# A convolution's transform with 90 in place of 98 rows, positions loaded in two halves, four units moved into a gap

## Chip, cores, metric

One core of one Trainium2 chip. The metric is the device time of one execution in microseconds (us). The kernel before takes 2610.57 us (median of four runs, 2609.2 to 2613.86). Almost all executions of one kernel agree within 0.3%.

## The reference, cut

```python
# x, v: (4, 12544, 128); pos_emb: (12544, 64); tokens for the second block: 4 * 12544
h_mlp  = np.maximum(pos_emb @ w1, 0.0) @ w2
window = np.exp(-0.01 * np.arange(S))[:, None]          # float32
h_filt = h_mlp * window
u = x * v;  L = 2 * S
y = irfft(rfft(u, L) * rfft(h_filt, L), L)[:, :S]       # causal convolution, per channel
x2 = (x * y).reshape(B * S, D)
h = np.maximum(np.maximum(x2 @ m1, x2 @ m2), x2 @ m3)   # 128 -> 768
out = h @ m_out                                         # 768 -> 128
```

In float32 the window is exactly zero from s = 10398 on. The filter therefore lives in 82 of the 98 blocks of 128 positions (82 x 128 = 10496).

## The kernel before: the parts that matter here

Four stages follow one another on one core. **Start:** a small network of the positions makes the filter (`mlp_in`, `mlp_out`). **First transforms** (`first_halves`): of the filter (512 passes over `spec`), then of batch 0 (32 units). **Pair loop**: a second product, a multiplication in the frequency domain and a third product for each pair of rows, batch 0 and the filter together. **Tiles**: 128 tiles, 32 a batch, each a last transform (`yps`) and six blocks of the maxout part (`pa`, `pb`, `ops`); the convolution of the next batch runs in 192 numbered slots beside the tiles of this one (`conv_steps`). "Pass" below means one matmul of the trace with its weight load; a matmul of the program is recorded as two of them (a transpose as one).

```python
NA = 64
halves = ((0, NA), (NA, NB))              # NB = 98: 64 blocks of positions, then 34
hs = spec[0:NB]...                        # the filter's values land in rows 0..97 of spec
def mlp_in(i):                            # 16 calls
    for q in range(8):
        for hf, (lo_, hi_) in enumerate(halves):      # the halves alternate
            nc.tensor.matmul(ps[lo_:hi_, q*FO:(q+1)*FO],
                posv[64*hf:64*hf+64, P-1-8*i-q, 0:hi_-lo_],   # stationary: 64 rows x 64 or 34 columns
                w1_sb[64*hf:64*hf+64], start=(q == 0), stop=True, ...)
def first_halves(ps, lhs, dst, copy):
    ...                                   # lhs: 98 rows x 64 columns; f1: 98 rows x 98 columns a pass
def conv_steps(b, per_unit, per_pair, lag):
    for u in range(0, NU, 2): s = int(u * per_unit) + 6 ...    # [cut]
    for g in range(NK):                                        # 49 pairs
        s = s0 + int(g * per_pair)
        at(s + lag[4], g_third, b, g); at(s, g_second, g)
        at(s + lag[0], g_butterfly, g); at(s + lag[1], g_swap, g); ...
# called with per_unit 1.9, per_pair 2.3, lag (1, 2, 3, 4, 5)
```

One slot is one such block of `pa`, `pb` and `ops`.

## Time and profile before

| Stage (span of the profiled run) | from, us | to, us | length |
|---|---|---|---|
| until the filter transform starts | 0 | 53.19 | 53.2 |
| filter transform | 53.19 | 74.90 | 21.7 |
| batch 0's units | 74.90 | 143.62 | 68.7 |
| pair loop and gap, to the first `pa` | 143.62 | 363.86 | 220.2 |
| tiles with the convolutions beside them | 363.86 | 2605.8 | 2241.9 |

The boundaries are starts of instructions in TensorE's timeline. In a profile line `64*34 64x64` are the rows and columns of the stationary part, then those of the moving part and the output. The prediction below shows the lines that its reading rests on. Two timeline lines (start, length, engine, line, what, count):

```profile
36.03 1.98 PE L262 MATMUL ps<-w_sb,specH 64*64 64x64 f32 x32
...
53.19 21.88 PE L124 MATMUL ps<-f,spec 98*64 98x98 f32 x512 [0.58 <-issue]
```

A run of 32 products of the positions takes 1.92 us from its start to the next instruction's, 60 ns a pass; longer runs take 56. The filter transform takes 42.7 ns a pass. The trace's first record of the clock is a rise at about 29.0 us. Ahead of that record the profile shows full clock for want of anything else. That the clock was half until then can be seen from one pair of passes in between, the `pw` product at 23.97 us: it took 0.75 us, and 0.45 us in run onepos (below), whose clock had risen at 22.9 us. So the products up to 29.0 us ran at half clock, 56 ns a pass, and they kept that pace after the rise.

### The profile page before, as it was taken

Reading aid. Unit: us, or ns where it says so; the run is one execution under the profiler, and the core shown is the slowest. Engines: PE = TensorE matmul, PEld = TensorE weight load, DVE = VectorE, ACT = ScalarE, POOL = GpSimd, SP = SyncE. Lnnn points to the kernel's source line nnn. Section 1 sums busy time; section 2 is a strip of 40 time slices with the busy share of each in tenths; the row PEclk is TensorE's granted clock in tenths of the full one; section 3 lists DMA queues with packets and bytes.
Section 4 is the critical chain, followed back from the end, with each engine's and each line's share of the span. In section 5 each row is a group of like instructions: output and inputs, shape, how many; then the busy total and the mean of one; then the engine's idle time right before and its main releaser. Section 6 shows DMA issues by size and latency. Waiting matters only on the chain. (4 is left out here: it accounts for less than half of the span.)

```text
span 2605.8 us, 63932 instructions
## 1 busy us (share of the span) xinstructions
PE 2550.6 (98%) x26937; PEld 1559.7 (60%) x26937; DVE 1332.1 (51%) x2670; ACT 1084.9 (42%) x2064; POOL 61.4 (2%) x120
## 2 busy tenths in 40 slices
PE   6999989999999999999999999999999999999999
PEld 6877756666665656666656555666565554444444
DVE  5678843336666643335666653335666652222222
ACT  1478843334445433334444533334444442222222
POOL 1012200000000000000000000000000000000000
PEclk9999989999999999999999999999999999999999
DMA  6668864456888844456888754455887852222221
GB/s 158 151 191 258 257 165 105 104 143 182 233 223 227 237 122 103 103 137 178 225 224 227 224 141 109 104 133 159 235 225 220 227 165 60 54 63 60 55 61 35
DMA packets 441504, 409.19 MB, mean 157 GB/s; under 512 B 292314, under 2 KB 343168, under 8 KB 441088
## 3 DMA queue, kind: packets, MB, share of 16 engines
q1 hardware_dynamic: 313856, 311.26, 45.1%
q10 hardware_dynamic: 121920, 78.64, 10.5%
q0 software_dynamic: 5440, 15.21, 2.3%
q8 instruction: 211, 3.46, 0.6%
q14 instruction: 77, 0.63, 0.1%
HBM read 315.07 MB, written 89.92 MB: 155 GB/s over the span
## 5 line engine op out<-in xcount | busy, mean ns | idle before, releaser
L437 DVE TENSOR_TENSOR hid<-hid,pb 128x392 f32<-128x392 f32 x768 | 431.6, 562 | 700.1 <-PE pb L115 565.1
L434 ACT ACTIVATE hid<-pa 128x392 f32<-128x392 f32 x768 | 382.4, 498 | 708.0 <-PE pa L115 642.6
L115 PE MATMUL pa<-gt,w_sb 128*64 128x392 f32 x3072 | 641.1, 496 | 11.8 <-ACT hid L434 11.0
L115 PE MATMUL pb<-gt,w_sb 128*64 128x392 f32 x3072 | 636.8, 493 | 1.2 <-DVE hid L437 0.6
L115 PE MATMUL ops<-hid,wo_sb 128*64 128x392 f32 x3072 | 635.8, 492 | 0.1
L115 PEld LDWEIGHTS pb<-gt,w_sb 128*64 128x64 f32 x3072 | 218.2, 136 | 290.5 <-issue 203.4
L115 PEld LDWEIGHTS ops<-hid,wo_sb 128*64 128x64 f32 x3072 | 220.2, 137 | 285.7 <-issue 284.9
L115 PEld LDWEIGHTS pa<-gt,w_sb 128*64 128x64 f32 x3072 | 196.2, 137 | 161.0 <-issue 115.8
L345 DVE TENSOR_TENSOR xt<-xt,ht 128x512 f32<-128x512 f32 x196 | 135.5, 692 | 196.0 <-ACT xs L340 148.3
L115 PEld LDWEIGHTS yps<-f,zt 98*64 98x64 f32 x4096 | 189.8, 137 | 55.2 <-issue 46.1
L115 PEld LDWEIGHTS ps<-ab,wt 128*64 128x64 f32 x3136 | 178.8, 137 | 68.7 <-issue 36.4
L115 PE MATMUL ps<-ab,wt 128*64 128x128 f32 x3136 | 212.6, 276 | 3.2 <-DVE ab L356 3.2
L368 ACT COPY zs<-ps 128x512 f32<-128x512 f32 x196 | 115.3, 588 | 236.9 <-PE ps L115 225.8
L115 PE MATMUL ps<-spec,wt 128*64 128x128 f32 x3136 | 204.6, 273 | 0.0
L124 PEld LDWEIGHTS ps<-f,uT 98*64 98x64 f32 x4096 | 183.4, 137 | 35.2 <-issue 30.5
L115 PE MATMUL yps<-f,zt 98*64 98x98 f32 x4096 | 196.7, 248 | 7.6 <-DMA zt<-zd 7.6
L124 PE MATMUL ps<-f,uT 98*64 98x98 f32 x4096 | 192.1, 248 | 1.9 <-ACT uT L300 1.4
L115 PEld LDWEIGHTS ps<-spec,wt 128*64 128x64 f32 x3136 | 179.5, 137 | 18.9 <-issue 18.9
L425 DVE TENSOR_TENSOR gt<-yps,xT 128x392 f32<-128x392 f32 x128 | 72.5, 567 | 171.6 <-PE yps L115 169.0
L339 ACT ACTIVATE xs<-xt 64x512 f32<-64x512 f32 x196 | 123.2, 628 | 77.7 <-DVE xt L140 45.4
L356 DVE TENSOR_TENSOR ab<-xt 128x256 f32<-128x256 f32 x392 | 148.1, 419 | 1.7
L128 DVE COPY spec<-ps 128x392 f32<-128x392 f32 x128 | 71.3, 566 | 135.3 <-PE ps L124 135.3
(62 smaller groups left out, 1685.1 us busy)
## 6 DMA issues: line engine op xcount, KB each, us to landing
wt<-wt_const SPq DMA_DIRECT2D x147, 512.0 KB
ht<-hd SPq DMA_DIRECT2D x294, 256.0 KB
zd<-zs ACTq DMA_DIRECT2D x196, 256.0 KB
zt<-zd SPq DMA_DIRECT2D x128, 392.0 KB
ut<-in_xr_dram SPq DMA_DIRECT2D x128, 196.0 KB
ut<-in_vr_dram SPq DMA_DIRECT2D x128, 196.0 KB
wt<-wt_const SPq DMA_DIRECT2D x98, 256.0 KB
xT<-in_x_dram SPq DMA_DIRECT2D x512, 49.0 KB
```

The costliest lines, as they stand in the source:

```text
L115: nc.tensor.matmul(out[64 * h:64 * h + 64], lhsT[:, 64 * h:64 * h + 64], rhs, start=start, stop=stop, skip_group_check=True)
L124: nc.tensor.matmul(ps[64 * c:64 * c + 64, (2 * i + r) * NB:(2 * i + r + 1) * NB], lhs[i][:, 64 * r:64 * r + 64], f1[:, c * NB:(c + 1) * NB ...
L128: copy(dst, ps[:, 0:4 * NB].rearrange("p (s r k) -> p k r s", s=2, r=2))
L339: nc.scalar.mul(xs[0:64], xt[64:128], -1.0)
L345: nc.vector.tensor_tensor(out=xt[:], in0=xt[:], in1=hts[g][:, 0], op=ALU.mult)
L356: nc.vector.tensor_tensor(out=ab[:, :, q, :], in0=y[:, :, 0, :], in1=y[:, :, 1, :], op=op)
L368: nc.scalar.copy(zs[:].rearrange("p k f -> p (k f)"), ps[:])
L425: nc.vector.tensor_tensor(out=g[:], in0=ps[:, 0:N], in1=xTs.pop(i)[:].rearrange("d p n -> d (p n)"), op=ALU.mult)
L434: nc.scalar.activation(h[:], pa[:, 0:N], Relu)
L437: nc.vector.tensor_tensor(out=h[:], in0=h[:], in1=pb[:, 0:N], op=ALU.max)
```

## The change

Because the filter is short, a circular transform of 2 x 90 x 128 points is enough where 2 x 98 x 128 stood. So a batch has 45 pairs for 49, and a pass of the first transform 90 columns for 98. The filter network is made for 82 blocks only. The positions are loaded in two halves so that the first products can start early. The first four units of batch 1 are computed in the gap ahead of the first tile. The rest of the convolution steps are spread over the slots more widely. The copy of `G` is halved. The core of the diff:

```diff
+N1 = 90
+NH = 82
-    NK = NB // 2
+    NK = N1 // 2
-    halves = ((0, NA), (NA, NB))
+    halves = ((0, NA), (NA, NH))                      # second half: 34 -> 18 blocks
-    hs = spec[0:NB]...
+    hs = spec[0:NH]...                                # filter transform: 98 -> 82 rows
-                        ps[..., (2 * i + r) * NB:(2 * i + r + 1) * NB],
-                        lhs[i][:, 64 * r:64 * r + 64], f1[:, c * NB:(c + 1) * NB],
+                        ps[..., (2 * i + r) * N1:(2 * i + r + 1) * N1],
+                        lhs[i][:, 64 * r:64 * r + 64],
+                        f1[0:lhs[i].shape[0], c * N1:(c + 1) * N1],
-    for hf, (lo_, hi_) in enumerate(halves):
-        (...).dma_start(pos[64*hf:64*hf+64, 0:(hi_-lo_)*P], posT[:, lo_*P:hi_*P])
+    for a in (64, 0):
+        for hf, (lo_, hi_) in enumerate(halves):
+            (...).dma_start(pos... [:, 0:hi_-lo_, a:a+64], posT... [:, lo_:hi_, a:a+64])
-            beside = conv_steps(b + 1, 1.9, 2.3, (1, 2, 3, 4, 5)) if b + 1 < B else {}
+                done = 4 if b == 0 else 0
+                beside = conv_steps(b + 1, done, 2.0, (174 - 2.0 * (NU - done)) / NK,
+                                    (1, 2, 3, 4, 5))  # a pair every 2.62 or 2.44 slots
+            for u in range(4):                        # ahead of the first tile
+                u_first(u)
# cut: loads, multiplications and turns of these four units late in the pair loop;
#      buffers; the halved copy of G
```

## The prediction

> **What bounds the kernel now.** I read the page first, then the groups of TensorE instructions with shapes kept apart, then the stretches, then the timelines of three places. The page says that TensorE (PE) is busy nearly always, that the start is the exception, and that the granted clock dips only around one slice:
>
> ```profile
> PE 2550.6 (98%) x26937; PEld 1559.7 (60%) x26937; DVE 1332.1 (51%) x2670; ACT 1084.9 (42%) x2064; POOL 61.4 (2%) x120
> PE   6999989999999999999999999999999999999999
> PEclk9999989999999999999999999999999999999999
> ```
>
> Busy time alone proves little for pipelined matmuls, so I took start-to-start times. In the last quarter, where only the tiles of the maxout part run, a block of 4 passes of 392 columns starts every 0.66 us and a block of 32 passes of 98 columns takes 1.36 us:
>
> ```profile
> 2304.64 0.83 PE L115 MATMUL ops<-hid,wo_sb 128*64 128x392 f32 x4
> 2305.30 1.53 PE L115 MATMUL yps<-f,zt 98*64 98x98 f32 x32
> 2306.66 0.83 PE L115 MATMUL pa<-gt,w_sb 128*64 128x392 f32 x4
> ...
> ```
>
> So a pass costs 164.4 ns at 392 columns and 42.5 ns at 98. In the middle stage, 16 passes of 128 columns take 0.875 us (54.7 ns each; blocks at 897.61, 898.48, 899.36). Everything is columns times 1/2.4 ns plus 1 to 2 ns. From 380 us to the end the waits of PE add up to only 12.2 us, so there **columns removed from PE are time removed**. The stretches show where this is not so:
>
> ```profile
> 0.00:75.00 75.00, 54.85 (x1047) 52.90 (x1049) 42.98 (x114) 14.02 (x27) 9.37 (x21) 1.00 0.60 146
> 75.00:280.00 205.00, 197.83 (x2994) 162.73 (x2992) 151.52 (x320) 149.79 (x260) 33.89 (x65) 1.00 0.75 212
> 350.00:352.00 2.00, 1.34 (x14) 1.30 (x16) 0.83 (x3) 0.00 (x0) 0.00 (x0) 0.50 0.77 197
> ```
>
> The columns after the length are PE, weight loads, VectorE (DVE), ScalarE (ACT), POOL, granted clock, DMA share, GB/s. Three places differ from the main stage: the start (first matmul at 14.3 us, a steady stream from 19.66 us, both waits on the positions), the loop over the transform's pairs (143 to 350 us), and a gap before the first tile, where the clock is halved as well. The timelines of one pair, and of the gap:
>
> ```profile
> 277.52 1.21 PE L115 MATMUL ps<-ab,wt 128*64 128x128 f32 x16
> 278.05 1.01 ACT L563 COPY ht<-sps 128x1024 f32<-128x1024 f32 x1
> 278.96 0.59 ACT L368 COPY zs<-ps 128x512 f32<-128x512 f32 x1
> 279.58 0.37 ACTq L369 DMA_DIRECT2D zd<-zs  x1
> 279.99 0.59 ACT L548 COPY G<-gps 128x512 f32<-128x512 f32 x1 [0.44 <-ACT zs L368]
> 280.47 0.38 ACT L145 COPY eo<-ps 128x256 f32<-128x256 f32 x1
> 280.87 0.63 ACT L339 ACTIVATE xs<-xt 64x512 f32<-64x512 f32 x1
> 281.51 0.62 ACT L340 COPY xs<-xt 64x512 f32<-64x512 f32 x1
> 281.63 1.21 PE L115 MATMUL ps<-ab,wt 128*64 128x128 f32 x16
> 282.15 1.01 ACT L563 COPY ht<-sps 128x1024 f32<-128x1024 f32 x1
> ...
> 353.29 0.37 ACTq L369 DMA_DIRECT2D zd<-zs  x1
> 360.22 2.88 PE L115 MATMUL yps<-f,zt 98*64 98x98 f32 x32 [7.59 <-DMA zt<-zd]
> 363.86 1.57 PE L115 MATMUL pa<-gt,w_sb 128*64 128x392 f32 x4 [0.76 <-DVE gt L425]
> ```
>
> ACT runs without a hole from 278.05 to 282.15 (its queue also issues a store): **this loop is bound by ACT at 4.10 to 4.11 us a pair**, although PE looks full. The first six pairs, which carry extra fold work on PE (0.58 us), take 4.54 us; without it PE would need 3.96 us a pair. That is PE's floor here. In the gap, PE has 7.6 us of waiting and runs at half clock from 350.0 to about 367.1 us.
>
> **What the Trainium skill says.** (1) "TensorE: Matmul & The Clock Gate", Back-to-back issue gap, gives N/2.4 + 2.5 ns for a warm matmul; the trace agrees in slope, with a smaller constant (42.5, 54.7, 164.4 ns at 98, 128, 392). (2) The same page, LDWEIGHTS, gives columns/1.2, which is 53 ns for 64 columns; if that bound, a pass of 98 columns could not take 42.5 ns with a 64-column load each. The trace decides against it, but no trace here shows a pass below 98 columns with packed weights, so a floor between 39 and 42 ns isn't excluded. (3) The same page, Part 1, has the clock halved after an idle window of about 3.4 us and restored after a busy one; the trace shows 0.50 from 350 to 367 us around the gap. (4) "DMA: Bandwidth & Descriptors", Why small descriptors are slow, charges about 3 cycles a packet on top of 32 B a cycle: 11 cycles for 256 B, 16 for 392 B (12.25 rounded up, plus 3). The 392 B loads of the input units moved 176 GB/s at a share of 0.74, which is 238 GB/s at full share; the positions in 256 B pieces should then reach about 225 GB/s as an estimate, not worse than the some 215 GB/s seen from 2 to 14 us.
>
> **The change part by part.**
>
> *Pairs, batches 1 to 3.* 45 in place of 49 pairs. A pair costs 2 x 0.875 = 1.75 us on PE. 3 x 4 x 1.75 = **21.0 us**.
>
> *First transform, batches 1 to 3.* Each unit has 32 passes, now 90 columns wide: 8/2.4 = 3.33 ns less each, 0.107 us a unit. 92 units that stay in this stage: 9.8 us. For the possible floor I count **9.4**. The last transform still makes 98 columns (only its contraction shrinks to 90 rows): nothing.
>
> *Pair loop of batch 0.* Four pairs less: 4 x 4.11 = 16.4 us. The copy of G halves from 512 to 256 elements: 0.59 to about 0.38 us, as the copy eo of that size; ACT falls to 3.90 us and PE at 3.96 takes over. I take 3.98, since two engines then run almost equally full: 39 pairs x 0.13 = 5.1. Together **21.5 us**.
>
> *The gap.* Before, from the start of the last third product (350.66) to the first pa (363.86) is 13.2 us, and 3.3 us of half clock follow (another 1.65 lost). The data path of the gap stays: copy, store, load back (353.29 to 360.22). Into it go four units: first transforms at 32 x 39.2 ns = 1.25 us plus one turn of 0.53, in all 5.5 us at full clock, and about 8 us if the clock is low at first. Both fit or nearly fit the wait. With the clock up by the first tile, third to pa becomes 10.7 to 12 us; the three earlier turns and four multiplications lengthen the tail of the loop by some 0.6. Gain of the gap itself **3 us**. The four units also leave the main stage: 4 x (1.35 + 0.53) = **7.5 us**.
>
> *Start.* 82 of 98 rows of positions: 2.7 in place of 3.2 MB, the first half being enough for the first eight products. At 225 GB/s the first half lands near 8 us and all near 14, so PE could start 8 to 11 us earlier. But ACT issues f4 as late as the positions land now (14.58, just after the first matmul), the window and its copies follow on ACT, and SP's first weight load is issued at 19.57 with an 18.2 us wait on the positions; VectorE needs it. So most of the early start meets other waits. I count **3.5 us**. Narrower weight loads (18 in place of 34 columns) in the products: **0.5**.
>
> *Filter transform and batch 0's units.* 512 passes from 42.7 to 39.4 ns: **1.6**. Sixteen double units at some 4.22 us: 0.21 less each would be 3.4, but VectorE waits there on input loads up to 3.8 us (PE 2 to 4 us in all), so **2**.
>
> *Fewer stalls* from the more even spacing of the conv steps (a unit every 2.0 slots for 1.9, a pair every 2.4 to 2.6 for 2.3): of 12.2 us of waits, **1**.
>
> Sum: 21.0 + 9.4 + 21.5 + 3 + 7.5 + 3.5 + 0.5 + 1.6 + 2 + 1 = 71.0 us. 2610.2 - 71.0 = **2539 us**, 2.7% less.
>
> **The rivals.**
>
> *A floor of the weight load takes over.* If a 64-column load sets a pass to 42.5 ns whatever the columns, all three first transforms gain nothing: 9.4 + 1.6 + 2 fall away, and about 0.4 in the gap. For it: the products of the positions take 56 ns at only 64 columns. Against: their weights are read with a stride of 128 elements, and 98, 128 and 392 lie on one line. Time then 2552.
>
> *The positions in small pieces are slower.* If descriptors are made at a fixed rate (the 392 B loads ran at some 450 packets a us), SP's 8192 pieces take 18 us; half lands near 11 and all near 20. The start then gains 0 to 3 us, and with any worse rate loses up to 5. Time 2539 to 2548. Opposite: if no other wait binds, the start gains 8 and the time is 2534.
>
> *DMA takes over the pair loop.* Its share is 0.86 to 0.89 at 4.11 us a pair; the same bytes in 3.96 us make 0.91. If it sticks at 4.11, 5 us are lost: 2544. Against: PE never waits for wt in this loop.
>
> *The gap keeps its clock low* and the late turns delay the chain: 3 us lost, 2542.
>
> **Range and chances.** The two largest terms (21.0 and 21.5) rest on counts and on PE's own measured pace and can hardly fail by more than 5 us together. The floor (13 us) I hold at one in eight, the start is uncertain by 5 us each way, gap and input phase by 3. Range 2526 to 2553. Within 2% begins above 2558, which needs the floor and a bad start together: 0.06. Slower would need something that no view shows: 0.01. Faster 0.93.
>
> **What would show it.** The group of uT passes: 128x90 shapes with 32 passes starting 1.25 us apart (1.35 refutes me). The pair loop: start of the third product every 3.96 to 4.0 us, G copied in 0.38, ACT no longer without a hole. The first stream of position products starting between 8 and 13 us, then a wait on ACT's window copies. The wait of yps on zt under 3 us, with clock 1.00 by the first pa. 45 pairs: 2880 passes in each ps group in place of 3136. From the first pa to the end some 40 us less than the 2242 before (21.0 + 9.4 + 7.5 + 1 and 1.65 of half clock). What would make me wrong above all: a new wait of PE in the pair loop or at the start, or passes of 90 columns that don't get shorter.

## More of the kernel before

ScalarE copies `eo` after a second product and `zs` after a third, makes `xs` in `g_swap` by two operations, and applies the relu to each `pa`. `pa` and `pb` share two PSUM buffers.

## The result, and the profile after

The changed kernel takes **2646.67 us** (median of four runs, 2645.75 to 2650.34). The ratio is 1.0139, interval 1.0121 to 1.0157: 1.4% slower, where 2.7% faster was predicted. Inside the 2% of the verdict that is "same", but the two sets of runs don't touch. (A ratio here is always the mean time of one kernel's fast runs over that of the kernel before's fast runs of the same rounds, so it isn't quite the ratio of the medians quoted.)

| Stage | before | after | difference | predicted |
|---|---|---|---|---|
| until the filter transform starts | 53.2 | 111.4 | +58.3 | -4.0 |
| filter transform | 21.7 | 38.4 | +16.7 | -1.6 |
| batch 0's units | 68.7 | 74.2 | +5.5 | -2.0 |
| pair loop and gap | 220.2 | 197.9 | -22.3 | -24.5 |
| tiles and convolutions | 2241.9 | 2223.8 | -18.1 | -38.9 |
| sum | 2605.8 | 2645.8 | +40.0 | -71.0 |

These are the two profiled runs. TensorE's busy time in the first part of the page rose although it does less work, and the rows of slices put nothing under suspicion:

```profile
PE 2590.7 (98%) x26329; PEld 1550.9 (59%) x26329; DVE 1275.2 (48%) x2558; ACT 1032.6 (39%) x1992; POOL 57.0 (2%) x112
...
PE   8989999999999999999999999999999999999999
...
PEclk9999999999999999999999999999999999999999
```

608 passes fewer (26937 to 26329) are busy for 40 us longer. So the passes themselves became slower somewhere, and an engine that is "busy" is no proof that it works at its pace. The timeline shows where:

```profile
60.64 5.97 PE L274 MATMUL ps<-w_sb,specH 64*64 64x64 f32 x32
66.54 1.09 PE L309 MATMUL pst<-eye,ut 128*98 128x128 f32 x4
...
111.44 38.67 PE L130 MATMUL ps<-f,spec 82*64 82x90 f32 x512 [0.56 <-issue]
149.87 7.26 PE L130 MATMUL ps<-f,uT 98*64 98x90 f32 x128
```

The products of the positions take 5.90 us for 32 passes, 184 ns each against 60 before. The filter transform takes 38.43 us for 512 passes: 75 ns each, which is 90 columns at 1.2 a ns, the half clock. The transposes of four passes in between also take 1.02 to 1.09 us where they took 0.57 to 0.65. The trace's first record of the clock is a rise at 154.3 us, so the whole start ran at half clock, although PE was busy nearly all the time. The page's PEclk row hides it, as the profile has nothing to show ahead of the first record.

The pair loop and the gap came out much as predicted. Two third products and the copy of `G` in the loop, then PE in the gap:

```profile
298.67 1.10 PE L121 MATMUL ps<-ab,wt 128*64 128x128 f32 x16
...
300.83 0.37 ACT L559 COPY G<-gps 128x256 f32<-128x256 f32 x1 [0.44 <-ACT zs L379]
...
302.63 1.05 PE L121 MATMUL ps<-ab,wt 128*64 128x128 f32 x16
```

```profile
410.77 1.17 PE L121 MATMUL ps<-ab,wt 128*64 128x128 f32 x16 [2.00 <-ACT uT L311]
412.63 1.46 PE L130 MATMUL ps<-f,uT 98*64 98x90 f32 x32 [0.69 <-ACT zs L379]
...
414.59 3.94 PE L130 MATMUL ps<-f,uT 98*64 98x90 f32 x96
419.78 1.57 PE L121 MATMUL yps<-f,zt 90*64 90x98 f32 x32 [1.25 <-DMA zt<-zd]
422.03 0.88 PE L121 MATMUL pa<-gt,w_sb 128*64 128x392 f32 x4 [0.67 <-DVE gt L436]
```

A pair takes 3.96 us here, 3.91 to 3.96 in the loop, for 4.11 before. The wait on `zt` is 1.25 us for 7.59; third product to first `pa` takes 11.26 us for 13.2. Blocks of 32 passes of 90 columns take 1.24 to 1.27 us, so there is no floor of the weight load.

In the tiles, the waits of PE grew (the engine waiting, for what; total us, times, longest). The kernel before, 380 to 2600 us:

```profile
PE pa L115 <- ACT hid L434: 11.0, 30, 0.6
PE pb L115 <- DVE hid L437: 0.6, 3, 0.2
```

The changed kernel, 440 to 2646 us:

```profile
PE pa L121 <- ACT hid L445: 14.0, 38, 0.5
PE pb L121 <- DVE hid L448: 8.9, 32, 0.5
```

A batch beside which a convolution runs takes 585.7, 593.3 and 594.5 us (start of its first `yps` to the next batch's) in place of 597.0, 598.3 and 597.2: 11.3 us less beside batch 1's convolution, of which 7.5 are the four units moved, and 5.0 and 2.7 us less for the later ones, where 10.4 us of passes were taken out of each. The passes did get cheaper as counted (first transforms 43.1 to 39.7 us a batch, second and third products 42.8 to 39.3 us each, start to start, beside the two later convolutions); `pa` rose from 128.3 to 133 us and `ops` from 133 to 135 us.

### The profile page after: what moved, and what is told of

Read it like the earlier page. It is cut to its first block, busy times and chain, and to the rows that moved or that the text cites. A ratio compares the mean times of both kernels' runs of the same rounds, so it can differ in the third digit from the quotient of the medians.

```text
span 2645.8 us, 62471 instructions
## 1 busy us (share of the span) xinstructions
PE 2590.7 (98%) x26329; PEld 1550.9 (59%) x26329; DVE 1275.2 (48%) x2558; ACT 1032.6 (39%) x1992; POOL 57.0 (2%) x112
## 5 line engine op out<-in xcount | busy, mean ns | idle before, releaser
L356 DVE TENSOR_TENSOR xt<-xt,ht 128x512 f32<-128x512 f32 x180 | 124.5, 692 | 242.9 <-ACT xs L351 199.9
L121 PEld LDWEIGHTS yps<-f,zt 90*64 90x64 f32 x4096 | 188.3, 136 | 48.9 <-issue 46.4
L121 PEld LDWEIGHTS ps<-ab,wt 128*64 128x64 f32 x2880 | 166.0, 137 | 54.7 <-issue 32.4
L121 PE MATMUL yps<-f,zt 90*64 90x98 f32 x4096 | 195.2, 247 | 1.3 <-DMA zt<-zd 1.3
L121 PE MATMUL ps<-ab,wt 128*64 128x128 f32 x2880 | 189.7, 274 | 3.4 <-ACT uT L311 2.0
L121 PE MATMUL ps<-spec,wt 128*64 128x128 f32 x2880 | 187.9, 273 | 0.0
L130 PE MATMUL ps<-f,uT 98*64 98x90 f32 x4096 | 184.3, 246 | 2.0 <-ACT uT L311 1.2
L121 PEld LDWEIGHTS ps<-spec,wt 128*64 128x64 f32 x2880 | 164.0, 137 | 7.8 <-issue 6.9
L367 DVE TENSOR_TENSOR ab<-xt 128x256 f32<-128x256 f32 x360 | 136.0, 419 | 1.6
L135 DVE COPY spec<-ps 128x360 f32<-128x360 f32 x128 | 67.3, 533 | 133.1 <-PE ps L130 133.1
```

The lines of the kernel that those rows point to most:

```text
L121: nc.tensor.matmul(out[64 * h:64 * h + 64], lhsT[:, 64 * h:64 * h + 64], rhs, start=start, stop=stop, skip_group_check=True)
L130: nc.tensor.matmul(ps[64 * c:64 * c + 64, (2 * i + r) * N1:(2 * i + r + 1) * N1], lhs[i][:, 64 * r:64 * r + 64], f1[0:lhs[i].shape[0], c * ...
L135: copy(dst, ps[:, 0:4 * N1].rearrange("p (s r k) -> p k r s", s=2, r=2))
L356: nc.vector.tensor_tensor(out=xt[:], in0=xt[:], in1=hts[g][:, 0], op=ALU.mult)
L367: nc.vector.tensor_tensor(out=ab[:, :, q, :], in0=y[:, :, 0, :], in1=y[:, :, 1, :], op=op)
```

## The experiments

The first theory: (A) the second half of the positions, now 18 columns wide, makes each product take longer; (B) the filter transform over 82 rows doesn't count enough as work to raise the clock; (C) the wider spacing of the steps puts more of ScalarE's work ahead of the relu. The rivals to A and B: the clock alone, low for want of a dense start; the loads of the positions in 256 B pieces. Single looks (one run, state unknown) served where the effect was tens of us, 3 rounds where a few us counted. Runs of the kernel before on the same chip all had medians between 2608.7 and 2611.6 us.

### A: the width of the second stationary

Runs w32 and w33 compute more blocks in the second half than the filter needs, 32 and 33 columns:

```diff
-    halves = ((0, NA), (NA, NH))
+    halves = ((0, NA), (NA, NA + 32))      # w32;  NA + 33 in w33
```

> The kernel after, with the second half of the position products 32 columns wide in place of 18 (96 rows of positions loaded; rows 82 to 95 are computed and never read). Theory, tile mode: up to 32 stationary columns PE uses a 32-column tile, above it a 64-column tile, and changing between the two drains PE; 32 columns then still cost about 0.73 us per four passes, and the time stays within 5 us of the kernel after (2640 to 2652). Rival, narrow loads: the cost falls gradually with the width, so 32 columns should be nearly as good as the 34 of the kernel before (about 0.22 us per four passes) and the time 70 us or more shorter. Rival, small DMA pieces disturb the reads of the positions: no change, since the pieces stay.

> The same with 33 columns, one more than in w32. Tile mode: both halves now use tiles of 64 columns, four passes take 0.22 to 0.23 us as in the kernel before, the position products end near 45 us in place of 111, the clock rises during them, the filter transform of 82 rows runs at about 39 ns a pass, and the time is 85 to 95 us below the kernel after, 2552 to 2565. Narrow loads: w32 and w33 within 2 us of each other. Small DMA pieces: both as slow as the kernel after.

Measured: w32 **2647.94 us**, w33 **2587.82 us**. One column is worth 60 us. The groups of the products in the third group's stretch (count, busy us, mean ns of one, idle before), w32 first, at 26 to 62 us, then w33, at 25 to 35 us:

```profile
L274 PE MATMUL ps<-w_sb,specH 64*64 64x64 f32 x95 | 22.9, 341 | 0.0
L274 PE MATMUL ps<-w_sb,specH 64*32 64x64 f32 x94 | 19.9, 313 | 0.0
```

```profile
L274 PE MATMUL ps<-w_sb,specH 64*64 64x64 f32 x93 | 10.5, 292 | 0.0
L274 PE MATMUL ps<-w_sb,specH 64*33 64x64 f32 x95 | 10.5, 275 | 0.0
```

Nearly as many passes (189 and 188) fill 36 us there and 10 us here: 190 ns a pass against 56, start to start. (The mean of one, 341 against 292, isn't the pace, since passes overlap.) The clock isn't the cause: of w33's first 62 passes (13.25 to 16.7 us) some 50 came ahead of the first rise of the clock at about 16.1 us, and they already ran at 55.5 ns. The loads of the positions are pieces of the same size in both.

The single records of the traces (third group; the views above merge them) show what is lost. In w33, as in the kernel before, the passes of the two halves run at the same time: a pass of each half starts every 108 to 111 ns, and the 33-column one follows its 64-column neighbour after 6 ns (median). In w32 and the changed kernel no two passes start together, and the pass after a change of width starts 237 to 246 ns after the one before it. Both a lost overlap and a cost of the change are thus in the 184 ns.

This fits what the Trainium skill says in "TensorEngine Tiling (Array Packing)", Key Properties: changing the tiling mode, and not just the tile, drains TensorE; its Available Configurations name both a 64x64 and a 64x32 mode. With 64 and 33 or 34 columns the two products alternate between tiles of one mode; with 18 or 32 columns every second pass would change the mode, as the two passes of one product follow each other. The traces show the step between 32 and 33 columns; that it is this drain is the reading which fits it, and isn't shown, since no record names the mode.

w33 missed its expectation, though: the filter transform stayed slow, at 74.9 ns a pass, and the stretches say why (length, busy and count of PE, weight loads, VectorE, ScalarE, POOL, then clock, DMA share, GB/s):

```profile
53.00:92.00 39.00, 38.77 (x518) 38.72 (x520) 20.75 (x51) 7.48 (x16) 4.72 (x9) 0.51 0.11 32
96.00:104.00 8.00, 7.62 (x150) 6.66 (x146) 5.27 (x14) 4.03 (x8) 0.65 (x1) 1.00 0.42 104
```

Now a record exists: the clock had been full and **fell** to half within this transform, while PE was busy for 38.77 of 39.00 us. But the fall itself came 0.4 us after the transform began (53.65 against 53.23 us), and run lag6 below, with 98 rows, has one at the same place (53.50 us). There the clock was back after 3.4 us; here it stayed at half for 41 us, to 94.6 us, 3.0 us after the units' passes of 98 rows began. So the fall isn't put down to the 82 rows, but the missing return is: theory B stands in that form.

Run grp18 keeps 18 columns but changes the width only once in a call, by the order of the loops (all of one half, then all of the other):

```diff
-        for q in range(8):
-            for hf, (lo_, hi_) in enumerate(halves):
+        for hf, (lo_, hi_) in enumerate(halves):
+            for q in range(8):
```

> The kernel after with 18 columns kept, but the eight products of the first half are issued first and then the eight of the second half, so PE changes its tile 2 times for each tile of 32 passes in place of 16. Tile mode: the cost is in the change, so the position products speed up by most of the loss: four passes in 0.24 to 0.40 us on average, time 2555 to 2600 (the clock may stay low). Narrow loads: a pass of 18 columns is slow by itself, no change from 0.73 us.

Measured: **2606.75 us**; products 118 ns a pass for 184 (0.47 us for four passes, above the 0.24 to 0.40 that I had expected), filter transform still 75.1. Fewer changes of width are indeed faster with the same widths, which speaks for a cost of the change. But 118 isn't 56. Run grp33, made later from the kernel with both repairs (w33f98 below), has this order with 33 columns, where no change of mode is left:

> The repaired kernel with the eight products of one half of the rows first and those of the other half after them, both second stationaries 33 columns wide. Earlier the grouped order with 18 columns took 118 ns a pass where the alternating order with 33 columns took 56. If the grouped order loses because two neighbouring matmuls on the same rows don't overlap: again 100 to 125 ns a pass, first products done some 25 to 30 us later, 2590 to 2600 us. If the 118 ns were only what was left of the changes between the widths: 56 to 65 ns a pass and 2565 to 2570 us.

Measured: **2585.7 us**, 20 us above w33f98, products 87 ns a pass in the third group, 101 in the short runs after it: a loss as expected, but a smaller one (100 to 125 ns and 2590 to 2600 us were forecast). The single records tell the parts. In grp18 a pass starts 107 to 112 ns (medians of the two halves) after the one before it within a half, never beside one of the other half, and 237 to 246 ns after it at a change of width; two changes in 32 passes make the 118. In grp33 the changes cost nothing, and neighbouring groups overlap at their borders, hence 87. So most of what grp18 left was the order itself, and a change of width costs some 130 ns. The Trainium skill, "TensorE: Matmul & The Clock Gate", Part 3: Packing small matmuls, states that a weight load overlaps with running matmuls only when its row group differs; alternating the halves gives that, grouping doesn't. This agrees: 56 ns alternating, 87 to 101 ns grouped, with equal widths. (All of grp33's products ran at half clock, but so did the first 50 passes of w33 at 55.5 ns.)

### B: the rows of the filter transform

Run f98 has the unchanged 18 columns, but its filter transform contracts over 98 rows again, the lower ones zero:

```diff
-    hs = spec[0:NH]...
+    hs = spec[0:98]...
+    nc.gpsimd.memset(spec[64:98]...[:, 0:FO * P], 0.0)
-                out=hs[:, :, r, 4 * i:4 * i + 4], ...
+                out=hs[0:NH, :, r, 4 * i:4 * i + 4], ...
```

> The kernel after, but the filter's first transform contracts over 98 rows (rows 82 to 97 cleared to zero by GpSimd) in place of 82. In the kernel after, it ran at 75 ns a pass, which is 90 columns at half clock, for 38 us of uninterrupted passes, and the clock rose 4 us after the passes of 98 rows began. Theory, activity: passes over 82 rows don't count enough to release the clock; with 98 rows the clock rises within 4 to 7 us of the start of the filter transform, its 512 passes take 22 to 24 us in place of 38.7 and the time is 12 to 18 us shorter, 2629 to 2635. Rival: the clock rises late for another reason (slow passes before it, or a fixed delay), and the filter transform stays at 75 ns.

Measured: **2627.4 us**; products 184 ns as in the changed kernel, filter transform 23.11 in place of 38.43 us. The clock rises at about 118.2 us, 6.7 us after that transform began. Zeros suffice; the number of rows counts, not the values.

Runs r96, r97 and r90 are f98 with 96, 97 and 90 rows. If the rows counted in groups of 32, 96 and 90 would be alike and 97 would be like 98.

> The kernel after with the filter's first transform contracting over 96 rows (rows 82 to 95 cleared), beside f98 with 98 rows, where the clock rose during that transform and its 512 passes took 23.1 us. Theory, activity is counted by groups of 32 rows, and four groups are needed with 64 columns: 96 rows are three groups, so the transform stays at half clock, 75 ns a pass, 38.4 us, and the time is within 4 us of the kernel after (2642 to 2650). Rival, activity grows smoothly with the rows and 98 is only above some limit: 96 rows are close to 98, and the clock rises as in f98 (about 23 us, time 2624 to 2632).

> The same with 97 rows. Groups of 32 rows: the 97th row brings in the fourth group, the clock rises within 7 us of the transform's start, it takes 22 to 24 us, and the time is 2624 to 2632. Smooth: r96 and r97 are alike.

> The kernel after with the filter's first transform over 90 rows (rows 82 to 89 cleared), between the 82 that left the clock at half and the 96 that raised it. My theory of groups of 32 rows has fallen with r96 (its clock rose). Theory now: the measure grows with the rows in use and has a limit between 82 and 96 for this stream; 90 rows fall on one side or the other, about 75 ns a pass and a time near the kernel after if below, about 44 ns and 2624 to 2632 if above. No side is forecast; a value between the two (a clock that rises late in the transform, 25 to 36 us for the 512 passes) would speak for a slow build-up in place of a limit.

| Rows | time, us | filter transform, us | first rise of the clock, us |
|---|---|---|---|
| 82 (changed kernel) | 2646.67 | 38.43 | 154.3 |
| 90 | 2642.39 | 38.42 | 152.6 |
| 96 | 2627.32 | 22.52 | 116.9 |
| 97 | 2628.82 | 23.10 | 118.3 |
| 98 | 2627.4 | 23.11 | 118.2 |

With 90 rows the rise comes 2.6 us after the units' passes of 98 rows began (149.97). So the groups of 32 fell as an idea; for this stream (64 columns of weights, 90 moving) the limit lies between 90 and 96 rows, by one run on each side. All four runs with 82 rows (the changed kernel, w32, w33, grp18) took 38.3 to 38.4 us. The products fit this too: in grp33, where passes over 64 rows follow one another, 44 us of them brought no rise (it came at 75.2 us, 5.1 us into the transform of 98 rows), while it came at 29.0 us in the kernel before, where passes of both halves, 64 rows each, run at once. In the prediction I had quoted that a busy window restores the clock; here 38 us of unbroken passes didn't. What exactly is measured stays open.

### Both repaired, and C: the spacing

Run w33f98 has 33 columns and 98 rows, the rest as changed. Run w33f98pace puts the spacing back too:

```diff
-    conv_steps(b + 1, done, 2.0, (174 - 2.0 * (NU - done)) / NK, ...)
+    conv_steps(b + 1, done, 1.9, 2.3, ...)
```

> The kernel after with both causes found so far undone: the second half of the position products 33 columns wide, the filter transform over 98 rows with zeros. If these two are all that was lost at the start, the position products end near 53 us as in w33, the filter transform takes 20 to 21 us in place of 38.3, and the input units follow at full clock: 17 to 20 us below w33's 2587.8, so 2567 to 2571, 1.5 to 1.7% below the kernel before. If the low clock of w33 had another cause that remains, it stays near 2588.

> w33f98 with the spacing of the steps beside the tiles as in the kernel before (1.9 slots a unit, 2.3 a pair). In the kernel after, third and second products of different pairs fall into one slot for 24 to 25 of 45 pairs (as counted from the schedule; 13 of 49 before), and PE's waits for ScalarE and VectorE to free the two banks of the tile part rose from 12.2 to 22.9 us, with more time in the tile part's blocks than these waits show (7 us a batch). Theory: the spacing causes it; the waits go back to about 12 us and the time is 12 to 20 us below w33f98, 2548 to 2557. Rival: the waits come from the smaller first transform and pairs themselves (less PE work to hide ScalarE behind); then w33f98pace stays within 4 us of w33f98.

The second of these texts contains a wrong count. Counted again, the third product of one pair and the second of another fall into one slot for 28 of 49 pairs before, for 33 of 45 (beside batch 0) and 38 of 45 (beside the others) after, and for 25 of 45 with the old spacing. Third product and swap share a slot for 14 of 49 before, 27 and 19 of 45 after, 13 with the old spacing.

Measured: w33f98 **2565.28 us** (2561.2 to 2568.45; ratio 0.9836, 0.9819 to 0.9852), filter transform 19.87 us or 38.8 ns a pass. w33f98pace **2543.01 us** (2541.64 to 2544.21; ratio 0.9746, 0.9732 to 0.9761). The spacing is worth 22 us. The waits went from 22.1 to 10.4 us, as expected. The waits of PE from the first tile on, w33f98 first:

```profile
PE pa L121 <- ACT hid L446: 13.3, 37, 0.4
PE pb L121 <- DVE hid L449: 8.8, 32, 0.5
```

```profile
PE pa L121 <- ACT hid L446: 10.4, 28, 0.9
```

How such a wait comes about is seen in the timeline of w33f98 (operations of ACT and the two blocks of `pa`):

```profile
834.13 0.83 PE L121 MATMUL pa<-gt,w_sb 128*64 128x392 f32 x4
...
834.35 0.58 ACT L380 COPY zs<-ps 128x512 f32<-128x512 f32 x1 [3.05 <-PE ps L121]
...
835.42 0.63 ACT L351 ACTIVATE xs<-xt 64x512 f32<-64x512 f32 x1 [0.49 <-ACT zs L380]
...
836.07 0.62 ACT L352 COPY xs<-xt 64x512 f32<-64x512 f32 x1
...
836.71 0.50 ACT L446 ACTIVATE hid<-pa 128x392 f32<-128x392 f32 x1
...
837.25 0.20 PEld L121 LDWEIGHTS pa<-gt,w_sb 128*64 128x64 f32 x4 [0.35 <-ACT hid L446]
837.26 0.88 PE L121 MATMUL pa<-gt,w_sb 128*64 128x392 f32 x4
```

The `pa` of 834.13 is done at 834.96. Its relu comes at 836.71, because `zs`, its store and both halves of `xs` stand ahead of it on ACT: a third product and a swap in one slot. Only the relu's end at 837.21 frees the buffer, and the next `pa` starts at 837.26; its weight load (`PEld`) bears the mark of the wait.

Which part of the spacing does it? Run pair23 puts back the pairs' spacing alone; run lag6 keeps the wide spacing and moves the third product one step later:

```diff
-    conv_steps(..., 2.0, (174 - 2.0 * (NU - done)) / NK, ...)   # pair23
+    conv_steps(..., 2.0, 2.3, ...)
-                                    (1, 2, 3, 4, 5))            # lag6
+                                    (1, 2, 3, 4, 6))
```

> The repaired kernel with one of the two spacings put back: pairs every 2.3 slots (as in the kernel before) in place of some 2.44 to 2.62, the units every 2.0 as changed. Coincidence of the third with the second product, or any property of the pairs' spacing, as the cause: 2541 to 2549 us, the whole of the 22 us. If the units' spacing of 2.0 (each unit at the same place of a slot pair) is the cause: 2560 to 2567 us.

> The kernel with both repairs (33 columns, transform over 98 rows, 2565 us) and its own wide spacing of the steps, but the third product of a pair one step later (lag 6 in place of 5). Counted in the schedule, the third product of one pair and the second of another then share a slot of the main stage for only 10 pairs of 45 beside the first batch and none beside the others (33 and 38 before), and third product and swap for 0 and 5 (27 and 19 before). If that coincidence makes ScalarE late for the relu: 2543 to 2553 us, with the waits of pa for ScalarE's hid and of pb for VectorE's hid well under the 13.3 and 8.8 us of the repaired kernel. If it is the spacing as such (where in a stretch of 128 matmuls the steps fall), nothing changes: 2562 to 2568 us.

Measured: pair23 **2542.77 us** (2541.11 to 2544.12; ratio 0.9744, 0.9728 to 0.976), the whole of the 22 us: the units' spacing plays no part. lag6 **2531.36 us** (2524.9 to 2532.78; ratio 0.9694, 0.9679 to 0.9709), better than I expected. From the first tile on, the wait of `pa` for the relu is nearly gone in lag6:

```profile
PE pa L121 <- ACT hid L446: 0.4, 2, 0.2
```

Its batches take 570.8, 583.0 and 582.9 us in place of w33f98's 585.5, 593.2 and 593.8. So the rival, that the wide spacing as such costs, is wrong: it is what lands on ACT together. The waits of the list are 21.7 of the 34 us; the blocks of `ops`, too, take some 6 us a batch less than in w33f98 (start to start), which no run explains. Lag 6 lessens both coincidences at once (third with second 10 and 0, third with swap 0 and 5), so which of the two weighs more isn't told by it.

Does the kernel before gain from the same number? Run before_lag6 changes only it there:

```diff
-            beside = conv_steps(b + 1, 1.9, 2.3, (1, 2, 3, 4, 5)) if b + 1 < B else {}
+            beside = conv_steps(b + 1, 1.9, 2.3, (1, 2, 3, 4, 6)) if b + 1 < B else {}
```

> The kernel before with one number changed: the third product of a pair six steps after its second product in place of five. Its own PE waits for ScalarE's relu come to 11.0 us from the first tile on. If the coincidence of third and second product in a slot (28 of 49 pairs before, some 5 with six) makes those waits, this kernel loses them and what hangs on them: 2595 to 2602 us, ratio 0.994 to 0.997. If the long lag helps only with the wide spacing of the changed kernel: 2607 to 2613 us.

Measured: **2609.42 us** (2604.72 to 2611.19), ratio 1.0002 (0.9985 to 1.0018): nothing. My expectation of 8 to 15 us was wrong. Its wait of `pa` for the relu fell from 11.0 to 4.6 us, but the blocks of second products took 45.3 in place of 42.8 us a batch (start to start). The coincidence of third and second falls to 5 of 49 there, but that of third and swap rises from 14 to 19. That fits the swap being the heavier part, as the timeline above has it, but it isn't shown. The lag pays only with the changed kernel's spacing.

### The gap and the start

Each of these three is w33f98pace with one part undone or moved. Run nogap takes the four units out of the gap. Run onepos loads each half of the rows in one piece, as before. Run early issues the loads of window, identity and backward matrix ahead of the positions.

```diff
-        if NK - 6 <= s < NK - 3: u_load(1, s - NK + 6)   # nogap: and the other three steps
-            for u in range(4): u_first(u) ...            # nogap
-                done = 4 if b == 0 else 0
+                done = 0                                 # nogap
-    for a in (64, 0):                                    # onepos
+    for a in (0,):                                       # onepos: whole rows of each half
+    nc.scalar.dma_start(win[:], ...); (eye); (back)      # early: moved ahead of this loop
     for a in (64, 0):
```

> w33f98pace without the part that puts the second batch's first four units into the end of the pair loop and the gap before the first tile. As predicted, that part is worth 7.5 us of work taken out of the main stage and about 3 us of the gap with its half clock: the time is 8 to 12 us above w33f98pace's 2543. Rival: the four turns and multiplications in the tail of the pair loop delay the chain to the first tile by as much as they save, and the difference is under 5 us.

> w33f98pace with the positions loaded in one piece for each partition half, contiguous as in the kernel before. In w33f98pace the first two groups of position products start at 10.4 us, but PE then waits 6.5 us for the identity matrix, which stands behind the positions in ScalarE's queue, and the third group starts at 24.65 us, as in the kernel before (24.64). Theory: the halving of the positions earns nothing there; onepos is within 2 us of w33f98pace. Rival: the 256 B pieces are a gain or a loss in transfer time; then the third group starts 3 us or more earlier or later, and the time follows.

> w33f98pace with the window, the identity and the reversal matrix issued ahead of the positions in ScalarE's queue. If the wait for the identity is what holds the start, the third group of position products starts near 18 us in place of 24.65; VectorE then waits for the first raw weights (used at about 26 us before), and PE can run at most 8 banks ahead, so that 2 to 5 us of it reach the end: 2538 to 2541. Rival: the positions finish later by as much, or the raw weights bind fully; then under 1.5 us.

Measured: nogap **2551.08 us** (2548.62 to 2556.38; ratio 0.9775, 0.976 to 0.9789): the gap's part is worth (0.9775 - 0.9746) x 2610 = 7.6 us, where 3 + 7.5 were predicted. In its trace the wait on `zt` is back at 8.1 us. onepos **2541.25 us** (2539.91 to 2544.1; ratio 0.9738, 0.9722 to 0.9754) and early **2541.23 us** (2540.12 to 2545.49; ratio 0.9737, 0.9723 to 0.9752): both no worse than w33f98pace. Loading the positions in halves earns nothing. In onepos the first product comes at 14.42 us in place of 10.41, but the third group of products starts at 24.11 us against 24.65: what stands behind the positions in the queues (identity, window) decides. In early the third group starts at 23.60, not near 18 as I had expected.

Run best has all that paid: lag6, onepos and early together.

> All that paid in one kernel: the change with 33 columns for the second half of the positions, the transform over 98 rows, the third product six steps after the second, the positions in one piece a half and the window, identity and backward matrix loaded ahead of them. From the 2531 us of the kernel with lag 6 and the 1 to 2 us that each rearrangement of the start brought: 2527 to 2532 us, ratio 0.968 to 0.970. If the start's rearrangements bring nothing together, since the raw weights come last either way: 2530 to 2533.

Measured: **2535.06 us** (2533.07 to 2538.03), ratio 0.9715 (0.9701 to 0.973): no better than lag6, and above the 2527 to 2532 us that I expected. The two rearrangements of the start don't add up: the third group of products starts at 27.50 us, against 24.80 in lag6, as PE waits for the positions for 22.2 us in all (counted from the start of the span), against 19.2 in onepos and 15.9 in early. The batches take the same 570.8, 582.9 and 582.9 us as in lag6. **The best kernel measured is lag6, 3% below the kernel before.**

## Why the prediction was wrong, by its own steps

**"Narrower weight loads (18 in place of 34 columns) in the products: 0.5" is the step that failed most.** It took the width for a matter of load time. The products took 184 in place of 56 to 60 ns, and with the start's other terms this stage ended 58.3 us later in place of 4 us earlier. w32 against w33 shows the cause to be the width of at most 32 columns beside one of 64: the passes of the two halves no longer run at once, and each change of width costs some 130 ns. The prediction didn't ask what 18 columns do beside 64.

**"Filter transform ... 512 passes from 42.7 to 39.4 ns: 1.6" failed too**, by 18 us. The 39.4 is right at full clock (38.8 in w33f98), but I carried the full clock over to a stream that contracts 82 rows. f98 shows that the rows decide. The low clock also reached 4.4 us into the units, part of the +5.5 there.

**"Fewer stalls from the more even spacing: 1" had the wrong sign.** The spacing lost 22 us (w33f98 against w33f98pace). I looked at how evenly steps are spread and didn't count which of them meet in one slot.

**"Start: 3.5" was not earned by the halves**: onepos, without them, is no slower. The prediction's own remark, that most of the early start meets other waits, should have been taken to its end.

**What held.** 45 pairs for 49 and narrower passes: second and third products fell by 3.5 us each and the first transform by 3.4 us a batch, 10.4 us together, near the 10.1 a batch that 21.0 and 9.4 make for three. The pair loop went to 3.91 to 3.96 us a pair (3.98 predicted), the copy of `G` to 0.37. The gap was worth 7.6 of 10.5. The rival of a weight-load floor was rightly held unlikely: no floor at 90 columns. With both traps and the spacing undone, w33f98pace took 2543 us, 4 above the predicted 2539. That it comes so near is in part luck. By stage, its trace against the kernel before's has the start at +0.2 us (-4.0 predicted), the filter transform at -1.9 (-1.6), the units at +0.7 (-2.0), pair loop and gap at -22.6 (-24.5) and the tiles at -42.4 (-38.9): what was missing ahead of the tiles was partly made up in them. None of the rivals named a pass that gets *slower*; "slower would need something that no view shows" was the sentence that should have warned me, for no view of the kernel before can show a shape that it doesn't contain.

**What stays open.** What exactly of 90 and 96 rows the clock's control sees; which coincidence on ACT weighs how much; why lag 6 makes the second products dearer in the kernel before.

## What to carry to other kernels

When a change makes an operand of TensorE smaller, ask first which shapes appear that the kernel before doesn't have, and whether they change the tiling mode between neighbouring passes or the activity that keeps the clock up; padding (33 for 18 columns, 98 for 82 rows of zeros) then is cheaper than the "saved" work. Where TensorE is busy in every slice, compare the time of one pass, start to start, with columns over the clock, and don't trust a clock row ahead of the trace's first clock record. When steps of two pipelines are interleaved, count which of them share a slot on the smaller engine; here one lag changed by one was worth 34 us in the repaired kernel, and nothing in the kernel before.

## What the Trainium skill lacked or had wrong

- "TensorEngine Tiling (Array Packing)", Key Properties, gives the drain no size, and the page doesn't say which mode a width between 32 and 64 columns has. Here 64 columns alternating with 18 or 32 took 184 to 190 ns a pass, with 33 or 34 took 56 ns. In grp18 a pass after a change of width started 237 to 246 ns after the one before it, others 107 to 112 ns: some 130 ns for each change, if it is this drain.
- "TensorE: Matmul & The Clock Gate", Part 1, speaks of busy time only. Here 512 unbroken passes over 82 or 90 rows didn't bring the clock up from half (0.51 with PE busy for 38.77 of 39.00 us), and 96 to 98 rows raised it within 5.5 to 6.7 us (r96, r97, f98).
- The same page, LDWEIGHTS, gives columns/1.2 as the time of a load, 53 ns for 64 columns. As a limit of the pace it doesn't hold here: passes of 90 columns with a load of 64 columns each took 38.8 ns throughout w33f98's filter transform.
- The same page, Part 3, has measured speedups for three tiles and more, none for two row groups of 64; here 56 ns a pass alternating and 87 to 101 ns grouped.
